# Batch 0's masks added on VectorE, batch 1's attention results on 64x64 places, and trace durations in the plan

## The chip, the cores and the metric

The kernel runs on one core of one Trainium2 chip. The core has five engines that work side by side: TensorE (matrix products), VectorE, ScalarE, GpSimd, and SyncE, whose queue issues the transfers (DMA). The metric is the time of one execution on the device in microseconds; a kernel's time is the median of its runs.

## The reference

Windowed attention over 8 batches, 8 heads, 576 tokens and a head size of 64, and then a two-layer network with a rational activation on the 4608 tokens of 512 values:

```python
scores = scale * q @ k.T                    # scale = 1/8
rel = pos[:, None] - pos[None, :]
mask_plain = (rel >= 0) & (rel < 32)        # heads 0 to 3
mask_dil = (rel >= 0) & (rel < 128) & (rel % 4 == 0)   # heads 4 to 7
attn = softmax(where(mask, scores, -1e9))
x = (attn @ v), heads side by side          # 4608 x 512
h = x @ w_in                                # 512 x 2048
P = a0 + a1*h + a2*h^2 + a3*h^3
Q = 1 + |b0|*|h| + |b1|*h^2
out = (P / (Q + 1e-6)) @ w_out              # 2048 x 512
```

q, k and v are 4-byte floats, the two weight matrices come as 8-byte floats.

## The kernel before

**Attention.** A batch is cut into six units (class `Unit`; three for the plain heads, three for the dilated ones, whose tokens are sorted by their residue so that each query sees a window of 32). A unit loads its q and k as one transfer of 448 KB (`load_qk`) and its v as one of 384 KB (`load_v`). Its scores are 24 small products for each half, 48 in all (`scores`), into columns 0 to 191 of a pair of PSUM banks: 64 rows of the array by 32 columns, moving 64 columns. The masks are a strip of 0 and -1e30 (`mask_t`, 96 KB, loaded once). For batches 0 and 1 (`on_pe`) the masks are written into the bank first, as products of an identity with the mask, and the scores are added to them; for the others VectorE adds the masks to the scores (`mask`, one or two additions a unit). Then come maximum, subtraction, exponential, sum, reciprocal (`max`, `sub`, `exp`, `sum`, `recip`) and a scaling on GpSimd (`norm`). All of batch 1's units subtract the maximum by a matmul (`KIND` 2, `sub_pe`), and one unit of batch 0 does it inside the exponential (`KIND` 1).

For batches 0 and 1 (`by_pe`) the probabilities are transposed on TensorE and copied back to SBUF (`transposes`, `place`). Later batches go through VectorE's 32x32 transposes and DRAM (`turn`, `put`, `move`).

The product with v (`av`) is again 48 matmuls, into columns 192 to 383 of a pair of banks. It has two forms. In batch 0 (`start`) v is the stationary operand: places of 64 x 64, 32 moving columns, and the result stands with the head's values on the partitions, as the network's first product needs it; `evac_hi` and `evac_lo` read it from the bank. In all other batches the probabilities are stationary: places of 64 x 32, 64 moving columns, and the result has to be turned: two 32x32 transposes on VectorE (`turn_out`), one store to DRAM (`put_out`) and four loads (`move_out`); then the evictions read the loaded tile.

An eviction splits a result into two parts, a high part `xh` (a ScalarE copy that rounds) and a low part `xl` (the difference). Both go into a batch's 512-token tiles. The last 64 tokens of a batch are left over; they go to DRAM and are worked on together as a ninth group. For batch 0's last two units (`LESS`) TensorE subtracts the high part in the bank (`less_hi`) and the low part is a copy.

Batch 0's units use three pairs of banks ("A", "B" and "att") for scores and results; the units from batch 1 on use "att" alone, for both. From batch 1 on a unit's scores are issued together with the `av` of the unit two before it, as one step of TensorE.

**Network.** 9 groups of 512 tokens by 16 slices of the inner 2048 give 144 tiles (class `Tile`). A tile has 12 matmuls of 128 x 512 for `h` (high and low parts of x and w_in), a chain of thirteen element-wise steps over ScalarE, VectorE and GpSimd (`abs` to `g_lo`), and 12 matmuls for `out`. The first eight tiles belong to batch 0, the next sixteen to batch 1, then come batch 0's other eight, and so on. Two banks hold `h`; a tile's `h` waits for the last read (`g2`) of the tile two before. Each of the 32 weight slices comes as a 512 KB transfer and is turned into a high and a low part by ScalarE, VectorE and GpSimd (`w_scale`, `w_low`, `w_join`, `w_hi`, `w_lo`).

**Order.** All steps are ops of a list scheduler (class `Plan`), which runs while the program is built. Each op has a duration for each engine that may take it, its predecessors and the buffers that it takes. At each step the plan picks, among the ops that can start within 200 ns of the earliest, the one with the lowest rank. Ranks count in tiles (`PERIOD`, 4743 ns): a network op's is its tile's number plus `LATE`, a unit's come backwards from `DUE`, a pair of numbers for each batch: the last unit's rank and the distance between units. `SLACK` moves loads and weights ahead or back. What comes out is one fixed order on each engine and on SyncE's queue; engines work in order, each instruction waiting for its predecessors by semaphores. The durations thus only decide the order.

The transfers of batch 0's units and the weights are chained in the order of their ranks. The coefficients (`lc`) and the masks (`masked`) have ranks -39.5 and -39.4 of their own.

Of the kernel before, what the change touches and what calls it, by code (L numbers as in the profile page):

```python
# [19 lines left out]
P = 128  # L20
# [18 lines left out]
DEPTH, LOADS, STAGE, AHEAD, ON_PE, BY_PE = 2, 2, 6, 6, 2, 2  # L39
# [39 lines left out]
class Plan:  # L79
# [6 lines left out]
    DMA_START, DMA_NS, DMA_RATE = 3300.0, 1750.0, 375.0  # L86
# [97 lines left out]
def tile_attention_moe(  # L184
# [72 lines left out]
    class Unit:  # L257
        def __init__(self, b, u):
            self.b, self.u, self.n = b, u, b * NU + u
            self.start, self.on_pe, self.by_pe = b == 0, b < ON_PE, b < BY_PE  # L260
            self.s_tag, self.o_tag = (START_S[u], START_O[u]) if self.start else ("att", "att")
            self.s, self.o_ps = two_banks(self.s_tag), two_banks(self.o_tag)
# [164 lines left out]
        def pieces(self):  # L427
# [14 lines left out]
            for s0, t0, step, num in segs:  # L442
# [14 lines left out]
        def src(self, cols):  # L457
            first, cnt = cols
            if not self.start:
# [4 lines left out]
        def dst(self, x, cols, d):  # L464
            return x[d].rearrange("p h (r t) -> p r h t", r=2) if self.start and cols[1] == 192 else x[d]
# [43 lines left out]
        def plan(self, by, tags):  # L509
# [10 lines left out]
            if prev:  # L520
                sc = op({"PE": 1320 + 300 * self.on_pe}, 0, lambda e: (prev.av(), self.scores()), *prev.placed, prev.lv, lq, *masks)
                clear = prev.finish(sc)
            else:
                sc = op({"PE": 1130 + 320 * self.on_pe}, 0, lambda e: self.scores(), lq, *masks)
# [5 lines left out]
            if kind == 2:  # L530
                mx = op({"DVE": 470}, 0, lambda e: self.max(True), ma)
                sb = op({"PE": 760}, 0, lambda e: self.sub_pe(), mx, identity)
                su = ex = op({"ACT": 480}, 0, lambda e: self.exp_s(), sb)
                sm = op({"DVE": 470}, 0, lambda e: self.sum(), ex)
# [3 lines left out]
            else:  # L538
                mx = op({"DVE": 470}, 0, lambda e: self.max(), ma)
                su = op({"DVE": 500}, 0, lambda e: self.sub(), mx)  # L540
                ex = op({"ACT": 425}, 0, lambda e: self.exp(), su)
                sm = op({"DVE": 470}, 0, lambda e: self.sum(), ex)
# [36 lines left out]
            if start:  # L579
                av = op({"PE": 1500}, 0, lambda e: self.av(), *self.placed, lv)  # L580
# [5 lines left out]
        def finish(self, av):  # L586
            b, start = self.b, self.start
            main, left = self.pieces()
            got = av
            if not start:  # L590
# [6 lines left out]
            low = {"DVE": sum(120 + 2 * c[1] / 0.96 for c, _ in main)}  # L597
            kl = lf = None
            if start:
                ms = eh  # L600
                if LESS[u]:
                    ms = op({"PE": sum(60 + 2 * c[1] / 1.6 for c, _ in main)}, 0, lambda e: self.less_hi(), eh, identity)
# [8 lines left out]
            else:  # L611
                low["POOL"] = sum(100 + 2 * c[1] / 0.49 for c, _ in main)
# [3 lines left out]
            if left:  # L616
                lf = op({"SP": 430 * len(left)}, self.by + 20.0, lambda e: self.put_left(), kl if start else got, dma=P * 2 * LEFT * 4 + 60000)
                left_done.append(lf)
                if start:
# [4 lines left out]
            else:  # L624
                plan.takes(got, "stage", STAGE, [x for x in (el, lf) if x])
# [8 lines left out]
            return [x for x in (el, kl) if x] if start else [to]  # L634
# [54 lines left out]
    def plan_weights(key):  # L689
# [4 lines left out]
        if wide:  # L694
            sc = op({"ACT": 600}, 0, lambda e: w_scale(key), f)
            lw = op({"ACT": 690, "POOL": 690}, 0, lambda e: w_low(key, e), f, consts)
# [350 lines left out]
```

## Time and profile before

| | |
|---|---|
| three runs | 913.51, 917.98, 916.32 us; median 916.32 |
| the profiled execution | 916.49 us, span 914.7 us |
| mean granted TensorE clock | 0.994 |
| busy share of the span | TensorE 97%, VectorE 81%, ScalarE 74%, GpSimd 51% |
| moved by DMA | 103.46 MB |

In the profile, PE is TensorE, PEld its weight loads, DVE VectorE, ACT ScalarE, POOL GpSimd, SP SyncE (SPq: its queue). L212 is the helper that issues every matmul, L209 the one for transfers, L215, L218, L221 and L224 those for activations, VectorE's and GpSimd's two-operand instructions, so the instructions are told apart by their tiles: `pair`, `pair_A` and `pair_B` are the banks of scores and results, `h` and `out` those of the network, `z` is a result that came back from DRAM, `y` a turned result on its way there, `l` the left-over columns. A row of the timeline is its start in us, its length, the engine, the instruction, its count, and in brackets the engine's idle time before it with what ended it. In grouped rows the busy us and the mean ns of one stand behind the bar.

### The profile page before, as it was taken

What the parts mean: (1) busy time and instruction counts of PE and PEld (TensorE: products, weight loads), DVE (VectorE), ACT (ScalarE), POOL (GpSimd) and SP (SyncE); (2) the same over time, 40 slices, a digit from 0 to 9 for tenths busy, and PEclk for the clock granted to TensorE, in tenths of its full rate; (3) what the DMA queues carried; (4) which work ended last, traced back from release to release, by engine and by line L of the source; (5) the groups of instructions that cost most, each with busy time, mean ns of one, the idle gap of its engine ahead of it and who ended that gap; (6) DMA issues with size and microseconds to landing.
All of it is one profiled execution on the core that took longest, in us unless ns stands there. A gap on an engine that the chain in (4) does not pass through costs nothing.

```text
span 914.7 us, 21129 instructions
## 1 busy us (share of the span) xinstructions
PE 883.2 (97%) x8153; PEld 716.1 (78%) x8153; DVE 742.3 (81%) x1312; ACT 675.4 (74%) x1092; POOL 467.7 (51%) x408
## 2 busy tenths in 40 slices
PE   5877999999999999999999999999999999999998
PEld 3755787887877878888888888888888788888876
DVE  4789999999988988788978888887779677566656
ACT  2676888877666777877787778677777688778764
POOL 2454554656635554555455555546455545444442
PEclk9989999999999999999999999999999999999999
DMA  9667460235633343334334324423333220001001
GB/s 359 240 221 249 154 234 1 99 124 190 198 99 110 110 134 118 119 111 125 115 113 127 121 83 146 129 82 85 115 95 91 61 69 1 1 1 47 0 1 47
DMA packets 85477, 103.46 MB, mean 113 GB/s; under 512 B 37376, under 2 KB 62848, under 8 KB 85376
## 3 DMA queue, kind: packets, MB, share of 16 engines
q1 hardware_dynamic: 85376, 102.11, 34.5%
q8 instruction: 64, 1.05, 0.5%
q14 instruction: 37, 0.30, 0.1%
HBM read 75.21 MB, written 26.87 MB: 112 GB/s over the span
## 4 chain that ended last, share of the span: by engine, by line
PE 75%; DVE 11%; DMA 5%; ACT 5%; issue 3%; POOL 1%; SPq 1%; DVEq 0%; POOLq 0%; ACTq 0%
PE out L212 34%; PE h L212 34%; PE pair L212 5%; DVE h L221 3%; DVE a L221 2%; DMA wi_raw<-in_w_in_dram 2%; ACT r L215 2%; DVE t L218 1%; DVE a L218 1%; DVE gl L218 1%; DMA wo_raw<-in_w_out_dram 1%; SPq L209 1%; DMA qk<-in_qk_dram 1%; ACT a L215 1%; PE pair_B L212 1%
## 5 line engine op out<-in xcount | busy, mean ns | idle before, releaser
L212 PE MATMUL h<-xh,wi 128*128 128x512 f32 x1136 | 378.1, 394 | 6.8 <-DVE a L221 6.5
L212 PE MATMUL out<-gh,wo 128*128 128x512 f32 x1136 | 353.8, 393 | 0.7 <-DVE os L218 0.7
L224 POOL TENSOR_TENSOR a<-r,a 128x512 f32<-128x512 f32 x121 | 156.6, 1294 | 241.1 <-ACT r L215 233.4
L212 PEld LDWEIGHTS h<-xh,wi 128*128 128x128 f32 x1136 | 214.5, 189 | 58.3 <-DVE a L221 12.6
L212 PEld LDWEIGHTS out<-gh,wo 128*128 128x128 f32 x1136 | 211.2, 188 | 45.9 <-DVE os L218 1.1
L212 PE MATMUL out<-gl,wo 128*128 128x512 f32 x568 | 221.8, 391 | 1.6 <-DVE gl L218 1.0
L212 PE MATMUL h<-xl,wi 128*128 128x512 f32 x568 | 222.4, 391 | 0.0
L224 POOL TENSOR_TENSOR gl<-a,gh 128x512 fp32r<-128x512 f32 x129 | 175.1, 1357 | 64.7 <-ACT gh L215 64.0
L221 DVE SCALAR_TENSOR_TENSOR h<-h,na_t,r 128x512 f32<-128x512 f32 x142 | 106.9, 753 | 111.0 <-ACT r L215 109.2
L215 ACT ACTIVATE r<-a,ln_bias 128x512 f32<-128x512 f32 x141 | 101.9, 723 | 82.8 <-POOL a L224 80.3
L215 ACT ACTIVATE r<-a,ab_t 128x512 f32<-128x512 f32 x141 | 114.7, 814 | 16.3 <-DVE a L221 14.5
L212 PEld LDWEIGHTS out<-gl,wo 128*128 128x128 f32 x568 | 106.6, 188 | 25.6 <-POOL gl L224 1.5
L212 PEld LDWEIGHTS h<-xl,wi 128*128 128x128 f32 x568 | 107.3, 189 | 21.5
L215 ACT ACTIVATE a<-h 128x512 f32<-128x512 f32 x140 | 83.5, 596 | 53.7 <-PE h L212 35.0
L215 ACT ACTIVATE t<-h,na_t 128x512 f32<-128x512 f32 x142 | 109.6, 772 | 5.0 <-PE h L212 4.6
L221 DVE SCALAR_TENSOR_TENSOR h<-t,na_t,h 128x512 f32<-128x512 f32 x142 | 107.3, 756 | 4.9
L215 ACT ACTIVATE r<-r,exp_bias 128x512 f32<-128x512 f32 x144 | 104.3, 724 | 4.7
L218 DVE TENSOR_TENSOR t<-t,h 128x512 f32<-128x512 f32 x142 | 96.6, 681 | 7.2 <-ACT t L215 7.1
L221 DVE SCALAR_TENSOR_TENSOR a<-a,r 128x512 f32<-128x512 f32 x141 | 100.2, 711 | 0.0
L221 DVE SCALAR_TENSOR_TENSOR a<-a,h 128x512 f32<-128x512 f32 x140 | 96.2, 687 | 4.8
L215 ACT ACTIVATE gh<-a 128x512 fp32r<-128x512 f32 x130 | 81.5, 627 | 23.2 <-PE out L212 14.9
L224 POOL TENSOR_TENSOR p<-p,sm 128x384 f32<-128x384 f32 x48 | 47.7, 993 | 34.3 <-DVE sm L352 28.1
(115 smaller groups left out, 712.4 us busy)
## 6 DMA issues: line engine op xcount, KB each, us to landing
qk<-in_qk_dram SPq DMA_DIRECT2D x48, 448.0 KB, 5.0
v<-in_vp_dram SPq DMA_DIRECT2D x48, 384.0 KB, 3.7
out_dram<-os SPq DMA_DIRECT2D x36, 256.0 KB, 2.3
wi_raw<-in_w_in_dram SPq DMA_DIRECT2D x16, 512.0 KB, 6.1
wo_raw<-in_w_out_dram SPq DMA_DIRECT2D x16, 512.0 KB, 6.9
results<-y SPq DMA_DIRECT2D x42, 192.0 KB, 2.4
z<-results SPq DMA_DIRECT2D x168, 48.0 KB, 2.5
turned<-u SPq DMA_DIRECT2D x36, 192.0 KB, 2.0
```

The lines of the kernel that those rows point to most:

```text
L209: pin(nc.sync.dma_start(dst, src))
L212: pin(nc.tensor.matmul(o, lhs, rhs, start=start, stop=stop, skip_group_check=free))
L215: pin(nc.scalar.activation(o, i, func, **kw))
L218: pin(nc.vector.tensor_tensor(o, x, y, op))
L221: pin(nc.vector.scalar_tensor_tensor(o, x, s, y, op0, op1))
L224: pin(nc.gpsimd.tensor_tensor(o, x, y, op))
```

## The change

- **Masks.** `on_pe` is now batch 1 alone. Batch 0's scores start without the mask products, and VectorE adds the masks to them, one or two additions a unit.
- **Batch 1's results.** A new flag `direct` (batches 0 and 1) takes the place of `start` in `av`, `pieces`, `src`, `dst` and `finish`. So batch 1's products with v use the 64x64 form, the results are split into `xh` and `xl` out of the bank, the left-over columns are copied out of it, and the transposes, the store and the loads of these six units are gone. Their low part can no longer go to GpSimd. The next scores in the pair of banks now wait for the low part and the left-over copy, where they waited for the two transposes.
- **Order of the first transfers.** The masks follow batch 0's first q and k; the coefficients, the first v and the second q and k follow the masks.
- **Plan.** Many durations are set to other values, near those of traced instructions, and the DMA model's three numbers are changed. `DUE`, `LATE` and `SLACK` have new values. `LESS` gets six zeros for batch 1.

```diff
-LESS = [0, 0, 0, 0, 1, 1]
-DUE = [(-41.16, 11.47), (-146.25, 19.43), (423.68, 72.57), (61.95, 5.87), (470.95, -17.55), (494.47, -17.25), (93.76, -24.29), (711.56, 21.96)]
-
-LATE = {"ab": -187.16, "ql": -342.11, "pl": -25.5, "qq": -118.36, "t1": -2.55, "t2": -120.77, "ln": 177.41, "ex": -496.7, "g0": -73.65, "g1": -54.63, "g2": -312.0, "gh": -189.38, "gl": 379.92, "out": 3.83}
-SLACK = {"sc": 2.49, "qk0": -51.8, "v0": -50.12, "load": 7.26, "wi": 11.43, "wo": -2.45, "w": -16.22, "gl": -5.19, "out": -6.13}
+LESS = [0, 0, 0, 0, 1, 1] + [0] * 6
+DUE = [(-96.65, 4.82), (-115.73, 29.97), (490.19, 66.11), (121.91, -6.01), (655.31, -16.58), (451.05, 0.82), (341.09, -38.16), (731.85, 36.31)]
+
+LATE = {"ab": -86.99, "ql": -477.5, "pl": 77.21, "qq": -192.99, "t1": -73.09, "t2": 3.35, "ln": 355.36, "ex": -377.4, "g0": -121.85, "g1": -6.11, "g2": -449.17, "gh": -159.19, "gl": 306.89, "out": 3.97}
+SLACK = {"sc": 2.52, "qk0": -58.23, "v0": -58.73, "load": 2.91, "wi": 1.92, "wo": -2.38, "w": -20.99, "gl": -8.34, "out": -4.45}
...
-DEPTH, LOADS, STAGE, AHEAD, ON_PE, BY_PE = 2, 2, 6, 6, 2, 2
+DEPTH, LOADS, STAGE, AHEAD, ON_PE, BY_PE, DIRECT = 2, 2, 6, 6, 2, 2, 2
...
-    DMA_START, DMA_NS, DMA_RATE = 3300.0, 1750.0, 375.0
+    DMA_START, DMA_NS, DMA_RATE = 1000.0, 1700.0, 380.0
...
-            self.start, self.on_pe, self.by_pe = b == 0, b < ON_PE, b < BY_PE
+            self.start, self.on_pe, self.by_pe, self.direct = b == 0, b == 1, b < BY_PE, b < DIRECT
...
-                        if self.start:
+                        if self.direct:
                             c0, c1 = 192 + 96 * h + 32 * i, P * i + 32 * g
                             mm(self.o_ps[64 * e : 64 * e + 64, r, c0 : c0 + 32], v_t[half, i, h, e], self.pT[half, c1 : c1 + 32], start=i == h == 0, free=True)
                         else:
...
-                    n = cnt if not self.start or cnt == 192 else min(cnt, 96 - first % 96)
+                    n = cnt if not self.direct or cnt == 192 else min(cnt, 96 - first % 96)
...
-                sc = op({"PE": 1320 + 300 * self.on_pe}, 0, lambda e: (prev.av(), self.scores()), *prev.placed, prev.lv, lq, *masks)
+                sc = op({"PE": 1320 + 700 * self.on_pe + 770 * prev.direct}, 0, lambda e: (prev.av(), self.scores()), *prev.placed, prev.lv, lq, *masks)
...
-                sb = op({"PE": 760}, 0, lambda e: self.sub_pe(), mx, identity)
+                sb = op({"PE": 950}, 0, lambda e: self.sub_pe(), mx, identity)
...
-            no = op({"POOL": 790}, 0, lambda e: self.norm(e), rc)
+            no = op({"POOL": 880}, 0, lambda e: self.norm(e), rc)
             if self.by_pe:
-                tr = op({"PE": 690}, 0, lambda e: self.transposes(), no, identity)
+                tr = op({"PE": 900 if start else 600}, 0, lambda e: self.transposes(), no, identity)
...
         def finish(self, av):
-            if not start:
+            if not direct:
                 to = op({"DVE": 590}, 0, lambda e: self.turn_out(), av)
                 po = op({"SP": 430}, 0, lambda e: self.put_out(), to, dma=P * 384 * 4)
                 got = op({"SP": 1800}, 0, lambda e: self.move_out(), po, dma=P * 384 * 4 + 160000)
...
-            if start:
+            if direct:
                 ms = eh
-                if LESS[u]:
+                if LESS[self.n]:
...
-            return [x for x in (el, kl) if x] if start else [to]
+            return [x for x in (el, kl) if x] if direct else [to]
...
-            ab = op({"ACT": 480}, k + LATE["ab"], lambda e: self.abs(), h)
+            ab = op({"ACT": 515}, k + LATE["ab"], lambda e: self.abs(), h)
...
-    lc = op({"SP": 60}, -39.5, lambda e: load(coef_t, coef), dma=3000)
-    masked.follows.append(lc)
+    lc = op({"SP": 430}, -39.3, lambda e: load(coef_t, coef), dma=3000)
...
+    masked.follows.append(first_loads[0])
+    for o in (lc, *first_loads[1:3]):
+        o.follows.append(masked)
```

More of the change, by code (lines that the diff above doesn't have):

```diff
@@ L458, in src @@
             first, cnt = cols
-            if not self.start:
+            if not self.direct:
                 return self.o[:, :384].rearrange("p (h t) -> p h t", h=2)[:, :, first : first + cnt]
@@ L464, in dst @@
         def dst(self, x, cols, d):
-            return x[d].rearrange("p h (r t) -> p r h t", r=2) if self.start and cols[1] == 192 else x[d]
+            return x[d].rearrange("p h (r t) -> p r h t", r=2) if self.direct and cols[1] == 192 else x[d]
         def evac_hi(self):
@@ L531, in plan @@
                 mx = op({"DVE": 470}, 0, lambda e: self.max(True), ma)
[L532 removed]
+                sb = op({"PE": 950}, 0, lambda e: self.sub_pe(), mx, identity)
                 su = ex = op({"ACT": 480}, 0, lambda e: self.exp_s(), sb)
[L534 removed]
+                sm = op({"DVE": 510}, 0, lambda e: self.sum(), ex)
             elif kind:
@@ L596, in finish @@
             eh = op({"ACT": sum(172 + 2 * c[1] / 1.4 * 0.75 for c, _ in main)}, 0, lambda e: self.evac_hi(), got)
-            low = {"DVE": sum(120 + 2 * c[1] / 0.96 for c, _ in main)}
+            low = {"DVE": sum(200 + 2 * c[1] / 0.9 for c, _ in main)}
             kl = lf = None
-            if start:
+            if direct:
                 ms = eh
-                if LESS[u]:
-                    ms = op({"PE": sum(60 + 2 * c[1] / 1.6 for c, _ in main)}, 0, lambda e: self.less_hi(), eh, identity)
+                if LESS[self.n]:
+                    ms = op({"PE": sum(150 + 2 * c[1] / 1.4 for c, _ in main)}, 0, lambda e: self.less_hi(), eh, identity)
                     ms.slack = 0.0
@@ L611, in finish @@
             else:
-                low["POOL"] = sum(100 + 2 * c[1] / 0.49 for c, _ in main)
+                low["POOL"] = sum(130 + 2 * c[1] / 0.45 for c, _ in main)
                 el = op(low, 0, lambda e: self.evac_lo(e), eh, lock=True)
@@ L616, in finish @@
             if left:
-                lf = op({"SP": 430 * len(left)}, self.by + 20.0, lambda e: self.put_left(), kl if start else got, dma=P * 2 * LEFT * 4 + 60000)
+                lf = op({"SP": 430 * len(left)}, self.by + 20.0, lambda e: self.put_left(), kl if direct else got, dma=P * 2 * LEFT * 4 + 60000)
                 left_done.append(lf)
-                if start:
+                if direct:
                     plan.takes(kl, "stage", STAGE, [lf])
@@ L624, in finish @@
             else:
-                plan.takes(got, "stage", STAGE, [x for x in (el, lf) if x])
+                if not direct:
+                    plan.takes(got, "stage", STAGE, [x for x in (el, lf) if x])
                 plan.takes(self.placed[0], *(("p", 2) if self.n % 2 else ("pT", 1)), [av])
@@ L695, in plan_weights @@
             sc = op({"ACT": 600}, 0, lambda e: w_scale(key), f)
-            lw = op({"ACT": 690, "POOL": 690}, 0, lambda e: w_low(key, e), f, consts)
-            jn = op({"DVE": 680}, 0, lambda e: w_join(key), sc, lw, lock=True)
+            lw = op({"ACT": 690, "POOL": 740}, 0, lambda e: w_low(key, e), f, consts)
+            jn = op({"DVE": 710}, 0, lambda e: w_join(key), sc, lw, lock=True)
             steps = [sc, lw, jn]
@@ L700, in plan_weights @@
             steps = [op({"DVE": 335}, 0, lambda e: w_copy(key), f)]
-        hi = op({"ACT": 550, "DVE": 460, "POOL": 620}, 0, lambda e: w_hi(key, e), steps[-1], lock=True)
-        lo = op({"DVE": 602, "POOL": 1280}, 0, lambda e: w_lo(key, e), hi, lock=True)
+        hi = op({"ACT": 550, "DVE": 460, "POOL": 680}, 0, lambda e: w_hi(key, e), steps[-1], lock=True)
+        lo = op({"DVE": 625, "POOL": 1350}, 0, lambda e: w_lo(key, e), hi, lock=True)
         plan.takes(steps[0], "stage", STAGE, [lo])
```

14 lines of the change are left out of this document (7 added, 7 removed).

## The prediction

> **What bounds the kernel now.** I read the busy shares first, then the engines by stretch, then the single lines of the stretches in which TensorE is not full.
>
> ```profile
> span 914.7 us, 21129 instructions
> PE 883.2 (97%) x8153; PEld 716.1 (78%) x8153; DVE 742.3 (81%) x1312; ACT 675.4 (74%) x1092; POOL 467.7 (51%) x408
> PE 75%; DVE 11%; DMA 5%; ACT 5%; issue 3%; POOL 1%; SPq 1%; DVEq 0%; POOLq 0%; ACTq 0%
> ```
>
> TensorE is busy for 883.2 of 914.7 us, and the chain of waits lies on it for 75%. So 31.5 us of TensorE's idle time are all that a better order can win, beside a faster clock and less work on TensorE. Where they lie, the engines by stretch show (length, then busy us of TensorE, its weight loads, VectorE, ScalarE, GpSimd; granted clock, DMA share):
>
> ```profile
> 0.00:40.00 40.00, 27.10 (x722) 21.71 (x722) 23.55 (x57) 17.70 (x50) 14.01 (x26) 1.00 0.78 285
> 40.00:80.00 40.00, 33.55 (x598) 26.18 (x598) 34.71 (x72) 26.07 (x46) 16.67 (x17) 0.91 0.79 274
> 80.00:120.00 40.00, 34.42 (x231) 26.78 (x230) 38.20 (x63) 34.65 (x58) 23.97 (x23) 0.96 0.45 148
> 120.00:200.00 80.00, 79.73 (x616) 63.75 (x615) 77.70 (x125) 66.09 (x106) 44.20 (x36) 1.00 0.32 112
> 300.00:400.00 100.00, 99.73 (x980) 81.25 (x979) 84.23 (x162) 75.31 (x121) 56.22 (x50) 1.00 0.40 122
> 900.00:915.00 15.00, 11.07 (x49) 8.82 (x47) 9.25 (x14) 4.68 (x7) 1.30 (x1) 1.00 0.19 72
> ```
>
> Of the idle time 24.9 us (12.9 + 6.5 + 5.6) lie before 120 us. After that TensorE is full until the last 14.7 us, where 3.6 us go to the last results. In the first 40 us no engine is full: VectorE idles 16.4 us, so the stage is set by waits. From 40 to 120 us VectorE is busy for 72.9 of 80 us (91%), and most of TensorE's stalls there end with one of its instructions:
>
> ```profile
> 48.34 0.72 PE L212 MATMUL pair<-v,pT 64*32 64x64 f32 x48 [2.46 <-ACT p L215]
> 51.69 1.65 PE L212 MATMUL pair<-mx,ident 128*128 128x192 f32 x4 [1.46 <-DVE mx L312]
> 61.08 0.92 PE L212 MATMUL pair<-mx,ident 128*128 128x192 f32 x4 [1.18 <-DVE mx L312]
> 89.19 0.50 PE L212 MATMUL h<-xh,wi 128*128 128x512 f32 x1 [3.35 <-DVE a L221]
> ```
>
> So what the change does before 120 us sets the time; whatever is saved there moves the full TensorE forward as a block. The working is made against the profiled execution, 916.49 us (span 914.7 and 1.8 us around it), which is 0.17 us above the median of 916.32.
>
> **The change, part by part. The first scores.** The queue of SyncE, its landings, and the first work that uses them:
>
> ```profile
> 0.72 0.38 SPq L209 DMA_DIRECT2D qk<-in_qk_dram  x1
> 1.16 0.42 SPq L209 DMA_DIRECT2D v<-in_vp_dram  x1
> 2.57 0.43 SPq L209 DMA_DIRECT2D mask_t<-in_mask_dram  x1
> DMA to landing us min/median/max: 3.2/6.2/10.2
> mask_t<-in_mask_dram SPq DMA_DIRECT2D x1, 96.0 KB, 4.7
> 7.31 0.48 PE L212 MATMUL pair_A<-mask_t,ident_b 128*128 128x192 bf16 x2 [7.31 <-DMA mask_t<-in_mask_dram]
> 7.72 0.97 PE L212 MATMUL pair_A<-qk 64*32 64x64 f32 x48
> 8.73 0.56 DVE L312 TENSOR_REDUCE mx<-pair_A 128x6 f32<-128x384 f32 x1 [1.43 <-PE pair_A L212]
> L218 DVE TENSOR_TENSOR pair<-pair,mask_t 128x192 f32<-128x192 f32 x36 | 13.0, 362 | 0.8
> ```
>
> The 3.2/6.2/10.2 us are the landings of batch 0's six q and k loads; the first takes 3.2 us from 0.72, so it is there at 3.9 us. TensorE waits on for the masks until 7.31, because the masks are the first matmuls of the unit. After the change the scores need q and k alone: 3.9 us, 1.0 us to the reduction's start (7.72 to 8.73), then the new mask additions (two of 0.36 us), so the first maximum starts at 5.6 instead of 8.73: 3.1 us earlier. If the masks, now issued in v's place at 1.16, take their 4.7 us again, they land at 5.9 and the maximum starts at 6.6 us: 2.1 us earlier. I take 2.6. The lower end is 0: the later units' loads arrive at the pace of the transfers (the largest landing is 10.2 us), and the head start may be lost there. The first v moves behind the masks by one issue of 0.43 us and is not used until the first unit's transposes are done, so this costs nothing.
>
> **Batch 0's masks on VectorE.** Six units issue six additions of 192 columns and three of 384 in place of twelve matmuls.
>
> ```profile
> L218 DVE TENSOR_TENSOR pair<-pair,mask_t 128x384 f32<-128x384 f32 x18 | 10.0, 556 | 0.0
> ```
>
> 6 x 0.362 + 3 x 0.556 = 3.8 us more on VectorE. TensorE loses 0.41 us for each unit (7.31 to 7.72), 2.5 us in all. In each unit's chain the one replaces the other, and VectorE's 16.4 idle us in that stage hide the sum, so I count 0; without that cover it costs 3.8.
>
> **Order of the loads.** The first units' ranks go 49 tiles forward for batch 0's last unit (its due time from -41.16 to -96.65, less 6.43 of slack), and the weights' go back by about 14 (4.77 and 9.51 of slack). Before, weights stood between them:
>
> ```profile
> 7.77 0.91 SPq L209 DMA_DIRECT2D wi_raw<-in_w_in_dram  x2
> 9.37 0.33 SPq L209 DMA_DIRECT2D qk<-in_qk_dram  x1
> 17.23 2.72 SPq L209 DMA_DIRECT2D v<-in_vp_dram  x3
> 24.29 0.97 PE L212 MATMUL pair<-qk 64*32 64x64 f32 x48
> ```
>
> Batch 0's last q and k are issued at 9.37, behind two weights, and with the longest landing of the six they are there at 19.6 us; of the three v loads from 17.23 the first is batch 0's last. Now all twelve come ahead of the first weight. The scores of that unit run only at 24.3 us (last line), since they follow the transposes of an earlier unit, so the loads alone did not hold it: what their order can win is bounded by TensorE's idle time of the first 40 us behind its first matmul, 12.9 - 7.3 = 5.6 us. What it can lose is one or two weights, 0.5 MB each at 285 GB/s (first stretch), 1.8 us each, when they are what the end of batch 0 waits for. I take 0.5 us gained, nearer to nothing, with 5.6 gained and 3.6 lost as the ends.
>
> **Batch 1 without its way through DRAM.** Away go two transposes for each unit, one store, four loads; the evictions read the bank.
>
> ```profile
> L413 DVE STREAM_TRANSPOSE y<-pair x12: 334/356/383, 42.3 to 98.0; 128x192 f32<-128x192 f32 x12
> L218 DVE TENSOR_TENSOR xl<-z,xh x7: 324/790/1370, 55.4 to 109.1; 128x256 fp32r<-128x256 f32 x3, 128x384 fp32r<-128x384 f32 x2, 128x96 fp32r<-128x96 f32 x1, 128x64 fp32r<-128x64 f32 x1
> L224 POOL TENSOR_TENSOR xl<-z,xh x2: 617/670/722, 88.9 to 89.5; 128x160 fp32r<-128x160 f32 x1, 128x192 fp32r<-128x192 f32 x1
> L218 DVE TENSOR_TENSOR xl<-pair_B,xh x4: 215/450/558, 19.0 to 27.7; 128x384 fp32r<-128x384 f32 x2, 128x192 fp32r<-128x192 f32 x1, 128x64 fp32r<-128x64 f32 x1
> L215 ACT ACTIVATE l<-pair_A x3: 198/198/238, 30.2 to 41.4; 128x32 f32<-128x32 f32 x3
> 107.77 1.91 DVE L218 TENSOR_TENSOR xl<-z,xh 128x64 fp32r<-128x64 f32 x2
> 109.58 0.68 DVE L221 SCALAR_TENSOR_TENSOR a<-a,h 128x512 f32<-128x512 f32 x1
> 110.32 0.50 PE L212 MATMUL h<-xh,wi 128*128 128x512 f32 x1 [1.21 <-DVE a L221]
> ```
>
> The transposes free 12 x 0.356 = 4.3 us of VectorE. Its subtractions were 7 x 0.79 = 5.5 us; now there are twelve pieces, all on VectorE and none on GpSimd (the pieces break at 96 columns): two at 0.55 and ten at about 0.35, some 4.6 us. That frees 0.9 more, 5.2 in all. Five copies of the left-over columns come new, 0.2 us each, on ScalarE or VectorE. VectorE is busy for 91% of this stretch and sets it, but a part of what it frees falls into its own idle time; the bounds are 0 and 5.2, and I take 0.8 of it: 4.1 us. The last lines show it: the low halves stand 1.9 us ahead of the multiplication that the next 128 x 512 matmul waits for. The latency of the way through DRAM I count at 0: batch 1's low halves end at 109.7, that multiplication at 110.3, so batch 1's readiness alone was not what TensorE waited for. Thirty issues fewer on SyncE, and 2.3 MB fewer, unblock the loads behind them; with the DMA share at 0.79 and below from 40 us on I count nothing.
>
> **Batch 1's products on 64x64 places.** One unit of each form, at the full clock, and one eviction that TensorE waits for:
>
> ```profile
> 36.45 0.90 PE L212 MATMUL pair_A<-pT,v 64*64 64x32 f32 x48
> 40.31 0.72 PE L212 MATMUL pair<-v,pT 64*32 64x64 f32 x48
> 19.58 1.50 PE L212 MATMUL pair_B<-pT,v 64*64 64x32 f32 x46 [1.22 <-DVE xl L218]
> ```
>
> 0.90 against 0.72 us, so 6 x 0.18 = 1.1 us more on TensorE; at the slow pace of the early stretch 1.50 (the third line) against 0.97 (48 matmuls of the 64x32 form at 7.72), up to 3.2. I take 1.1. The Trainium skill, TensorEngine Tiling (Array Packing), section Instruction Overhead, says that a matmul of fewer than about 60 columns costs as much as one of 60. By it, half as many places at a time and 32 columns instead of 64 would make the unit twice 0.72 us and the total 913.6 instead of 910.4 us (an estimate); the trace's 0.90 us, which is no doubling, decides.
>
> **Reordering of the rest.** The plan's durations and ranks change for all tiles. From 120 to 900 us TensorE idles for some 3.0 us (31.5 less 24.9 and 3.6; the stretch 300 to 400 above has 0.27), so there is nearly nothing to win and something to lose: bounds -2 and +5, taken as 0. The tail likewise 0.
>
> **Sum:** 916.5 - 2.6 - 0.5 - 4.1 + 1.1 = 910.4 us.
>
> **Rivals.** *The bank is held too long (slower).* Batch 1's scores and results share one pair of banks. Before, two transposes freed the results; now ScalarE's copy, VectorE's subtraction and the left-over copy must be through before TensorE may write the next scores, and TensorE is in order: all tiles' matmuls behind those scores wait too. Batch 0 shows the price once: 1.22 us until the subtraction was done. For six units that is 7.3 us, and the 1.1 us for the larger places; with the 2.6 us of the start still gained it ends at 922.3. It decides from the point where the eviction ends later than the reading of the scores that ran beside it. Against it: the units of batch 1 came some 10 us apart (transposes from 42.3 to 98.0 for six units), while a subtraction takes 0.56 us at most (558 ns above). Chance 0.16.
>
> *VectorE's sum binds (no change).* If VectorE is the bound from the first scores on, its new 3.8 us count and its 5.2 us are nearly given back: 1.4 us gained, less 1.1 on TensorE: 916.2; with half of the start's 2.6 us kept 914.9. For it speaks the 91%; against it 16.4 idle us before 40. The change not doing what it says belongs here: were the second q and k load what batch 0 waits for, the masks' place would be worth nothing. Chance 0.18.
>
> *The first stage closes up (faster still).* All of batch 0's data are there early, and the first stage's idle time shrinks by half of the 5.6 us, 2.8, VectorE's full 5.2 us count, and the gap of 3.35 us ahead of 89.19 goes with the slow clock after it. The first three give 916.5 - 3.1 - 2.8 - 5.2 + 1.1 = 906.5; with half of the 3.35 us gap beyond VectorE's share 904.8. Chance 0.16.
>
> **How the numbers follow.** My forecast has 0.50. A measurement of this kernel can tell about 0.5% from no change, so faster ends at 911.7 and slower begins at 920.9. The forecast's own range is 906 to 915, and about seven tenths of its chance lie below 911.7. Faster: 0.36 and the last rival's 0.16, together 0.52. Same: the rest of the forecast, 0.14, and nearly all of the 0.18: 0.31. Slower: the bank's 0.16, and 0.01 for a reordering that costs its 5 us on top of a bound VectorE: 0.17. The range for 8 in 10 goes from 902 (the last rival with its 2 us from the later reordering) to 921, which leaves out most of the slower case.
>
> **What would show it.** Right: the first scores near 4 us and the first maximum near 6; batch 0's six q and k loads all ahead of the first weight; VectorE's share from 40 to 120 us below 91% or the same work ending some 5 us sooner; the stalls at 61 and 89 us shorter. Wrong: TensorE idle ahead of batch 1's scores with the subtraction or the left-over copy as the releaser; TensorE idle for more than 3 us between 120 and 900; the first 128 x 512 matmul not before 41.9 us, where it begins now.
>
> ```profile
> 41.89 0.50 PE L212 MATMUL h<-xh,wi 128*128 128x512 f32 x1
> ```

## The result, and the profile after

The kernel after takes 924.99 us (median of eight runs, 920.88 to 929.41) against 915.94 for the kernel before (eight runs beside it, 913.51 to 918.58): ratio 1.0101, 95% interval 1.0084 to 1.0119. It is slower, by 9.3 us (0.0101 of 916), where 910.4 was forecast; differences below that rest on a ratio are worked out like this one. The profiled execution took 925.27 us. Its page and the engines by stretch (length, then busy us of TensorE, its weight loads, VectorE, ScalarE, GpSimd; granted clock, DMA share, GB/s):

```profile
span 923.5 us, 21101 instructions
PE 889.1 (96%) x8141; PEld 721.6 (78%) x8141; DVE 726.1 (79%) x1296; ACT 675.4 (73%) x1097; POOL 481.4 (52%) x427
PE 75%; DVE 6%; ACT 4%; DMA 3%; POOL 1%; issue 1%; SPq 1%; ACTq 0%; POOLq 0%; DVEq 0%
```

```profile
0.00:40.00 40.00, 26.06 (x705) 20.92 (x706) 25.56 (x64) 20.03 (x51) 14.11 (x26) 1.00 0.89 324
40.00:80.00 40.00, 33.03 (x569) 25.65 (x568) 29.26 (x60) 27.05 (x59) 20.16 (x21) 0.92 0.71 232
80.00:120.00 40.00, 38.32 (x255) 30.89 (x254) 36.69 (x61) 35.09 (x61) 25.25 (x23) 0.99 0.37 134
120.00:200.00 80.00, 79.30 (x617) 63.81 (x616) 74.89 (x122) 64.92 (x103) 51.54 (x43) 1.00 0.31 104
200.00:300.00 100.00, 96.90 (x960) 78.45 (x959) 86.67 (x163) 66.96 (x108) 48.42 (x48) 0.98 0.44 137
300.00:400.00 100.00, 98.43 (x1062) 79.40 (x1061) 82.20 (x158) 73.62 (x119) 54.73 (x48) 1.00 0.40 124
400.00:500.00 100.00, 98.85 (x976) 80.32 (x976) 81.42 (x154) 74.32 (x118) 53.72 (x47) 1.00 0.37 115
```

Three things are to be seen. VectorE did get lighter, 742.3 to 726.1 us, and from 40 to 120 us its share fell from 91% to 82% (29.26 + 36.69 of 80). That did not put TensorE ahead: by 120 us it has done the attention of the same units in both kernels, but only 201 recorded 128x512 matmuls where it had done 211; at one in 0.23 us that is 2.3 us behind. And behind 120 us holes have come: 0.7, 3.1, 1.6 and 1.2 us in the last four rows, with a lower clock in one of them. The kernel before has 0.3, 1.8, 0.3 and 0.0 us there; of its four rows these two have not been shown yet:

```profile
200.00:300.00 100.00, 98.16 (x1060) 78.55 (x1059) 90.16 (x169) 71.64 (x116) 51.34 (x49) 1.00 0.49 155
400.00:500.00 100.00, 100.00 (x983) 81.80 (x982) 85.20 (x158) 75.43 (x121) 54.22 (x44) 1.00 0.38 116
```

So of the 8.8 us by which the span grew (914.7 to 923.5) some 6.5 lie behind 120 us, where none of the moved work is left. At 250 us both kernels have done 729 of these matmuls (the kernel after one unit's scores fewer); at 400 us it is 1298 against 1325, which is 6.2 us. Most of the loss falls between these two points.

TensorE's timeline of the early part (start, us, matmuls; in brackets the idle time ahead and what ended it):

```profile
3.91 0.97 PE L212 MATMUL pair_A<-qk 64*32 64x64 f32 x48 [3.91 <-DMA qk<-in_qk_dram]
...
7.88 0.97 PE L212 MATMUL pair<-qk 64*32 64x64 f32 x48 [3.00 <-DMA qk<-in_qk_dram]
...
16.18 0.86 PE L212 MATMUL pair_B<-pT,v 64*64 64x32 f32 x21 [2.40 <-issue]
...
47.12 1.65 PE L212 MATMUL pair<-mx,ident 128*128 128x192 f32 x4 [1.12 <-ACT xh L215]
...
48.32 0.88 PE L212 MATMUL h<-xh,wi 128*128 128x512 f32 x1
...
53.52 0.90 PE L212 MATMUL pair<-pT,v 64*64 64x32 f32 x48
...
57.75 0.92 PE L212 MATMUL pair<-mx,ident 128*128 128x192 f32 x4 [1.91 <-DVE xl L218]
```

VectorE's and SyncE's timelines:

```profile
5.72 0.56 DVE L312 TENSOR_REDUCE mx<-pair_A 128x6 f32<-128x384 f32 x1
```

```profile
16.21 0.33 SPq L209 DMA_DIRECT2D wo_raw<-in_w_out_dram  x1
```

The first scores start at 3.91 us and the first maximum at 5.72, as forecast, but the second unit's wait 3.00 us for their q and k, and the first 128x512 matmul comes at 48.32 instead of 41.89 us. In batch 1 the softmax now waits for evictions out of the same pair of banks (47.12 and 57.75).

The largest hole behind 120 us, on TensorE, in the chain of waits and in SyncE's queue:

```profile
256.74 0.94 PE L212 MATMUL pair<-v,pT 64*32 64x64 f32 x44 [3.08 <-DMA pT<-turned]
```

```profile
251.65 5.04 DMA pT<-turned
...
256.74 1.58 PE pair L212 x74
258.32 4.38 PE h L212 x12
...
266.55 2.95 PE h L212 x12
```

```profile
248.19 0.38 SPq L209 DMA_DIRECT2D turned<-u  x1
248.61 1.44 SPq L209 DMA_DIRECT2D os<-part  x3
250.21 0.88 SPq L209 DMA_DIRECT2D left<-z  x2
251.14 0.47 SPq L209 DMA_DIRECT2D turned<-u  x1
251.65 1.25 SPq L209 DMA_DIRECT2D pT<-turned  x2
```

Three fetches of partial sums (256 KB each) are issued between a unit's store of transposed probabilities and the load that brings them back; that load takes 5.04 us, and the twelve matmuls behind the hole take 4.38 us instead of 2.95.

### The profile page after: what moved, and what is told of

Same layout as the page of the kernel before. It is cut to its first block, busy times and chain, and to the rows that moved or that the text cites. A ratio compares the mean times of both kernels' runs of the same rounds, so it can differ in the third digit from the quotient of the medians.

```text
span 923.5 us, 21101 instructions
## 1 busy us (share of the span) xinstructions
PE 889.1 (96%) x8141; PEld 721.6 (78%) x8141; DVE 726.1 (79%) x1296; ACT 675.4 (73%) x1097; POOL 481.4 (52%) x427
## 4 chain that ended last, share of the span: by engine, by line
PE 75%; DVE 6%; ACT 4%; DMA 3%; POOL 1%; issue 1%; SPq 1%; ACTq 0%; POOLq 0%; DVEq 0%
PE h L212 36%; PE out L212 35%; PE pair L212 4%; ACT r L215 2%; DVE a L221 2%; DVE h L221 2%; DMA z<-results 1%; SPq L209 1%; DMA results<-y 1%; POOL a L224 1%; DVE t L218 1%; DMA pT<-turned 1%; ACT t L215 1%; ACT a L215 0%; ACT xh L215 0%
## 5 line engine op out<-in xcount | busy, mean ns | idle before, releaser
L224 POOL TENSOR_TENSOR gl<-a,gh 128x512 fp32r<-128x512 f32 x133 | 179.2, 1347 | 44.6 <-ACT gh L215 41.9
L215 ACT ACTIVATE gh<-a 128x512 fp32r<-128x512 f32 x126 | 79.1, 628 | 27.5 <-PE out L212 20.5
L224 POOL TENSOR_TENSOR p<-p,sm 128x384 f32<-128x384 f32 x48 | 44.6, 930 | 34.0 <-DVE sm L352 31.3
```

Source lines behind the costliest of these rows:

```text
L215: pin(nc.scalar.activation(o, i, func, **kw))
L224: pin(nc.gpsimd.tensor_tensor(o, x, y, op))
```

## The experiments

Two theories stood against each other: that the loss lies in the **parts** of the change (F in the expectations), or in the new **written-out order** of all tiles (E). All ratios are to runs of the kernel before on the same chip; 0.001 is 0.92 us.

**x1: one spot of the order.** Three of the four fetches of partial sums go behind the next load of transposed probabilities; nothing else moves.

```diff
+        first = named["part"][:3]
+        at = self.order.index(first[-1])
+        behind = next(o for o in self.order[at:] if getattr(o, "name", None) == "move")
+        for o in first:
+            self.order.remove(o)
+        at = self.order.index(behind) + 1
+        self.order[at:at] = first
```

> The changed kernel with one thing moved: three of the four loads that fetch batch 0's partial sums back (256 KB each) are issued behind the loads of the next unit's transposed probabilities instead of ahead of them; every other engine keeps its order. Theory A (the order that the new ranks gave costs the time behind 120 us): the stall of 3.08 us at 256.7 us, and the slow clock behind it (12 matmuls of h in 4.38 instead of 2.95 us), go: 3 to 5 us faster than the changed kernel, 920 to 922 us. Rival B (the time is lost in the first stage, and later stalls only take up slack that another wait would take): within 1.5 us of the changed kernel's 925.

920.09 us, 1.0052 [1.0034, 1.0071]: 4.5 us of the 9.3 are gone with three transfers. TensorE's timeline at the place:

```profile
254.53 0.65 PE L227 MATMUL pair<-v,pT 64*32 64x64 f32 x42 [0.33 <-DMA pT<-turned]
```

**x2 and z4: the evictions out of the shared banks.** Batch 1's evictions go behind the exponential of the unit that shares the banks. In x2 this also moved the last two units' evictions behind the first network matmuls that read them: that version reads those parts of x before they are written. z4 moves batch 1's own units alone (the condition `b == 1`).

```diff
+        for ex, evict in self.pairs:
+            at = self.order.index(ex)
+            early = [o for o in evict if self.order.index(o) < at]
+            for o in early:
+                self.order.remove(o)
+            at = self.order.index(ex) + 1
+            self.order[at:at] = early
...
+            if prev and prev.direct and b == 1:
+                plan.pairs.append((ex, prev.evictions))
```

> The changed kernel with batch 1's evictions (high part, low part, left-over copy) moved behind the exponential of the unit whose scores share the pair of banks; TensorE's order is unchanged. Theory C (in the changed kernel the eviction and the softmax of that pair of banks wait for each other in turn: high part after the maximum, subtraction after the high part, low part after the subtraction, exponential after the low part): TensorE's waits of 1.12 us at 47.1 and 1.91 us at 57.8 go, the exponentials start about 1.5 us earlier each, 2 to 4 us faster, 921 to 923 us. Rival D (the next scores then wait for the eviction instead): the waits reappear ahead of the next scores, 925 or more.

> The kernel after with the evictions of batch 1's own units alone moved behind the exponential of the unit that shares the banks; the order on TensorE and GpSimd is the same. Theory C (the wait of the exponential for the low part is what costs before 120 us): 921 to 923 us against 925, with TensorE's stalls of 1.1 and 1.9 us at 47 and 58 gone. Rival D (the bank is then held longer, and the next scores wait instead): 925 us or more, with new stalls ahead of batch 1's results or scores that end with the subtraction.

x2: 926.56 us, 1.0105 [1.0057, 1.0153]; z4: 923.60 us, 1.0090 [1.0060, 1.0120], neither apart from the kernel after, and z4 lies between what its two theories gave. The waits did not go, they moved ahead of the next results. TensorE in x2:

```profile
55.72 0.90 PE L224 MATMUL pair<-pT,v 64*64 64x32 f32 x48 [1.55 <-DVE xl L230]
...
73.04 0.90 PE L224 MATMUL pair<-pT,v 64*64 64x32 f32 x48 [1.77 <-ACT l L227]
```

**v3: x1 and z4 together.**

```diff
+        first = named["part"][:3]
...
+        for ex, evict in self.pairs:
...
```

> The kernel after with the edits of x1 (three part-sum fetches behind the next pT loads) and z4 (batch 1's evictions behind the exponential) together. If the two costs are separate: 925.0 - 4.9 - 1.4 = 918.7 us. If the waits only give way to the next in line: 920 us, as x1 alone. Not below before in either case, if batch 1's part costs 2 to 3 us by itself as w2 has it.

922.17 us, 1.0051 [1.0035, 1.0067], as x1 alone (1.0052): the second edit gave nothing more.

**x3: the order alone.** The kernel before, its due times nudged at random by about 0.3 of a tile; the same work.

```diff
-DUE = [(-41.16, 11.47), (-146.25, 19.43), ...]
+DUE = [(-41.38, 11.54), (-146.53, 19.47), ...]
-LATE = {"ab": -187.16, "ql": -342.11, ...}
+LATE = {"ab": -187.17, "ql": -341.48, ...}
```

> The kernel before, with every rank moved by some 0.3 of a tile at random (DUE and LATE) and nothing else changed; the plan's own end goes from 907.3 to 918.9 us. Theory E (the times of both kernels are set by how well the ranks were fitted to their plan, and any other fit costs several us): 922 to 930 us, stalls of TensorE behind 120 us or a longer first stage. Rival F (the order matters little, the parts of the change matter): 914 to 918 us.

924.80 us, 1.0108 [1.0084, 1.0133]. Another order of the same work is worth the whole result.

**x4: the kernel after with the ranks of the kernel before** (DUE, LATE and SLACK).

```diff
-DUE = [(-96.65, 4.82), (-115.73, 29.97), ...]
+DUE = [(-41.16, 11.47), (-146.25, 19.43), ...]
...
```

> The changed kernel, its new durations kept, with the ranks (DUE, LATE, SLACK) of the kernel before; the plan's own end goes from 911.5 to 922.2 us. Theory E (fit of the ranks): 930 to 938 us, more than either kernel. Rival F (the parts of the change cost the time, the ranks little): 922 to 928 us. If the new ranks are the bad part: 912 to 918 us.

931.88 us, 1.0189 [1.0149, 1.0229]. The ranks fit one set of durations; with the new durations the old ranks are worse still.

**y0 to y3: every version with ranks searched anew.** The durations of the kernel after in all four, and ranks from equally long searches; without the parts, with the masks alone, with batch 1's results alone, with both. The ranks shown are y0's; each has its own.

```diff
-    DMA_START, DMA_NS, DMA_RATE = 3300.0, 1750.0, 375.0
+    DMA_START, DMA_NS, DMA_RATE = 1000.0, 1700.0, 380.0
...
-DUE = [(-41.16, 11.47), (-146.25, 19.43), ...]
+DUE = [(-43.35, 5.23), (-116.64, 77.9), ...]
```

> None of the change's parts but its durations: the program's steps are those of the kernel before, the plan has the new durations, and DUE, LATE and SLACK were searched anew from the ranks of the kernel before for the plan's own end (912.8 us by it). One of four kernels with the same search and the same starting ranks. Theory E (the fit of the order sets the time; the parts are worth 2 us or less each): all four within some 5 us of each other, and the plan's own ends (912.8, 916.3, 912.3, 913.7) don't foretell which is first; this one 918 to 926. Rival F (the parts themselves cost the 9 us): this one 913 to 917.

> Batch 0's masks on VectorE and the new order of the first loads alone, batch 1's results as before; the same durations and the same search (plan's own end 916.3). Theory E: within 5 us of the one without the parts, 920 to 928. Rival F, if the masks are the costly part: 5 to 9 us above the one without.

> Batch 1's results on 64x64 places and out of the bank alone, masks and first loads as before; the same durations and search (plan's own end 912.3). Theory E with the chain in the bank pair (which the plan does not know): 1 to 4 us above the one without, 919 to 929. Rival F, if this is the costly part: 5 to 9 us above. If the DRAM way's removal is worth my predicted 4 us: 3 to 4 us below it.

> All parts of the change, the same durations and search (plan's own end 913.7), another fit than the changed kernel's. Theory E: 918 to 930, several us from the changed kernel's 925 either way although nothing but ranks differs. Rival F: 923 to 927.

922.54 (1.0060 [1.0044, 1.0076]), 924.12 (1.0079), 923.89 (1.0068) and 925.81 us (1.0093 [1.0073, 1.0113]). With an order found in the same way, both parts together cost 3.3 us (925.81 - 922.54), and the order of y0 by itself, without any part, costs 5.5 us. How much of the 3.3 us is the luck of four searches no run tells: the nudge of x3 alone moved the time by 9.9 us.

**z1 and w1: the masks in the old order.** The kernel before with its ranks and durations; each addition goes right ahead of its unit's maximum, the mask matmuls are dropped, the load is second. w1 also moves the scaling of the coefficients, which in z1 stood first on VectorE, behind the first subtraction (the last pair of lines).

```diff
-            on_pe = self.on_pe
+            on_pe = self.on_pe and not self.start
...
-    mx = op({"DVE": 470}, 0, lambda e: self.max(), ma)
+    mx = op({"DVE": 470}, 0, lambda e: (self.start and self.mask(), self.max()), ma)
...
             load(t, qk[self.n])
+            if self.n == 0:
+                load(mask_t, mask)
...
-    su = op({"DVE": 500}, 0, lambda e: self.sub(), mx)
+    su = op({"DVE": 500}, 0, lambda e: (self.sub(), self.n or make_na()), mx)
```

> The kernel before with its plan's numbers and so its written-out order untouched; only batch 0's masks move to VectorE in place (each addition right ahead of the maximum of its unit, the twelve mask matmuls dropped) and the masks' load goes from the fifth to the second transfer. Theory 1 (the forecast's term of the first scores holds when nothing else is reordered): 2.6 us less than before, 913.3 against 915.9, with the first scores at 4 us. Theory 2 (the head start is lost before 120 us whatever the order, as in the kernel after): within 1.5 us of before, with TensorE's idle time before 120 us again at 22 us or more.

> As the run z1 (the kernel before in its own order, batch 0's masks on VectorE, their load second), and the scaling of the coefficients, which stood first on VectorE and held its first mask addition until the coefficients landed at 8.4 us, moved behind the first unit's subtraction. Theory 1 (in z1 only that instruction hid the head start): the first maximum near 6 us and the end 2.1 to 2.6 us below before, 914.0 to 914.5 against 916.6. Theory 2 (the second unit's q and k land at 8.2 us and take the head start anyway): the first maximum near 6 us, but the second unit's scores at 8.2 us as in z1, and the end within 1.5 us of before.

z1: 916.68 us, 0.9995 [0.9981, 1.0010]; w1: 916.72 us, 1.0009 [0.9994, 1.0025]: nothing, with the first scores more than 3 us earlier. The page of w1 and its TensorE:

```profile
PE 880.4 (96%) x8141; PEld 714.9 (78%) x8141; DVE 745.7 (82%) x1321; ACT 675.0 (74%) x1092; POOL 466.0 (51%) x408
```

```profile
3.73 0.97 PE L212 MATMUL pair_A<-qk 64*32 64x64 f32 x48 [3.73 <-DMA qk<-in_qk_dram]
...
8.41 0.97 PE L212 MATMUL pair<-qk 64*32 64x64 f32 x48 [3.71 <-DMA qk<-in_qk_dram]
...
12.74 0.96 PE L212 MATMUL pair<-qk 64*32 64x64 f32 x48 [1.15 <-DMA qk<-in_qk_dram]
...
28.91 0.65 PE L212 MATMUL pair_A<-pT,v 64*64 64x32 f32 x16 [2.77 <-issue]
...
41.68 0.50 PE L212 MATMUL h<-xh,wi 128*128 128x512 f32 x1
```

The head start is handed back at the second and the fourth unit's loads and in a stop of 2.77 us without a releaser; the first 128x512 matmul comes 0.2 us earlier than before.

**z2 and z3: batch 1's results in the old order, as it was meant.** The evictions stand where the transposes stood.

```diff
-    to = op({"DVE": 590}, 0, lambda e: self.turn_out(), av)
+    to = op({"DVE": 590}, 0, lambda e: self.evict() if self.direct else self.turn_out(), av)
...
-    po = op({"SP": 430}, 0, lambda e: self.put_out(), ...)
+    po = op({"SP": 430}, 0, lambda e: self.direct or self.put_out(), ...)
```

> The kernel before with its plan's numbers and order untouched; only batch 1's results run on 64x64 places and are evicted out of the bank, high part, low part and left-over columns together at the place where the transposes stood. Theory 1 (the forecast's two terms, -4.1 and +1.1): 913 us. Theory 2 (the bank held by the chain of maximum, high part, subtraction, low part, exponential costs some 1.2 us a unit and the larger places 1.1 us): 916 to 922 us, with TensorE's stalls before batch 1's work ending with the copy or the subtraction of the pair of banks.

> Both parts in the kernel before with its plan's numbers and order untouched. Theory 1 (the forecast's terms add: -2.6, -4.1, +1.1): 910.3 us, which would put the whole loss on the new plan. Theory 2 (the parts themselves cost, or gain nothing): 915 to 922 us. In the refitted plans the two parts came to +3.3 us together.

927.19 us, 1.0116 [1.0101, 1.0132], and 929.41 us, 1.0141 [1.0125, 1.0156]. The numbers look like Theory 2, but the stalls don't lie in batch 1. TensorE in z2:

```profile
200.76 0.50 PE L212 MATMUL h<-xh,wi 128*128 128x512 f32 x1 [2.17 <-DVE a L221]
...
252.12 0.87 PE L212 MATMUL pair<-v,pT 64*32 64x64 f32 x42 [2.10 <-DVE sm L349]
```

The condition of both expectations was not met: the pieces of 96 columns changed the durations of batch 1's evictions in the plan, and with them the order of some 400 lines of VectorE's 1219. By 120 us TensorE is even ahead in z2, 221 of the 128x512 matmuls against 211 in the kernel before, with the attention of the same units done; then 15.5 us of idle time follow, where the kernel before has 6.6.

**w2 and w3: the same in the true old order.** The plan costs the evictions as before, so only batch 1's own instructions differ (with `plan` set, `pieces` gives the old pieces for batch 1); w3 has w1's edits as well.

```diff
-        def pieces(self):
+        def pieces(self, plan=False):
+            direct = self.direct and not (plan and self.b)
...
-            main, left = self.pieces()
+            main, left = self.pieces(True)
```

> As the run z2, but with the plan's durations of batch 1's evictions held at their old values too: the pieces of 96 columns had changed them in z2, and the plan had laid out some 400 of VectorE's 1219 lines otherwise, so z2 had not kept the order as its expectation said. Here only batch 1's own instructions differ. Theory 1 (the forecast's -4.1 and +1.1): 913.6 us against 916.6. Theory 2 (the bank pair's chain costs by itself): 918 to 924 us. Theory E (z2's 10.6 us were its new order): well below z2's 927.2, within 3 us of before.

> w1 and w2 together: every part of the change in the order of the kernel before. Theory 1 (all of the forecast's terms): 910.9 us against 916.6. Theory E with Theory 2 of w1: within 3 us of before. Theory 2 of w2: 918 us or more.

w2: 919.02 us, 1.0029 [1.0014, 1.0043]; w3: 919.89 us, 1.0039 [1.0024, 1.0054]. The same work as z2 and z3, 8.0 and 9.3 us faster by its order. The time of w2 fits its Theory 2 and its Theory E alike. The parts cost 3.6 us in the old order, and their interval lies clear of the 1.0084 where that of the kernel after begins: of the 9.3 us, 5.7 are left for the new order, if the two add. What w2's 2.7 us are, the engines in the stretch of 42 to 92 us show, first of the kernel before, then of w2, and w2's page and TensorE's timeline:

```profile
42.00:92.00 50.00, 39.27 (x526) 30.37 (x527) 44.74 (x84) 35.66 (x63) 22.30 (x24) 0.91 0.72 245
```

```profile
42.00:92.00 50.00, 39.16 (x530) 30.30 (x517) 38.69 (x73) 33.34 (x63) 19.73 (x20) 0.88 0.60 207
```

```profile
PE 885.5 (97%) x8153; PEld 718.8 (78%) x8153; DVE 736.6 (80%) x1305; ACT 675.0 (74%) x1100; POOL 465.9 (51%) x406
```

```profile
49.31 1.44 PE L212 MATMUL pair<-pT,v 64*64 64x32 f32 x48 [2.75 <-ACT p L215]
...
53.73 1.65 PE L212 MATMUL pair<-mx,ident 128*128 128x192 f32 x4 [1.64 <-DVE mx L313]
...
64.55 0.92 PE L212 MATMUL pair<-mx,ident 128*128 128x192 f32 x4 [1.75 <-DVE mx L313]
...
66.31 0.90 PE L212 MATMUL pair<-pT,v 64*64 64x32 f32 x48
...
92.40 0.79 PE L212 MATMUL h<-xh,wi 128*128 128x512 f32 x1 [4.09 <-DVE a L221]
```

VectorE works 6.1 us less there, and TensorE idles as long as before (10.8 against 10.7 us). Four waits at the same places are longer, 2.75, 1.64, 1.75 and 4.09 us where they were 2.46, 1.46, 1.18 and 3.35; three others that ended with VectorE are shorter or gone, 0.68 us for 1.11 near 80 us and none for 1.00 at 83.24 and 1.21 at 110.32. Over the whole span 2.3 of the 2.7 us are TensorE's busy time (885.5 against 883.2) and 0.4 us its idle time; the granted clock in this stretch was 0.88 against 0.91.

Where VectorE's freed time went, its waits from 42 to 112 us show (us in total, times, longest), first of the kernel before, then of w2:

```profile
DVE xl L218 <- ACT xh L215: 0.6, 2, 0.5
```

```profile
DVE xl L218 <- ACT xh L215: 8.3, 5, 2.4
```

The low parts now stand in VectorE's line where the transposes stood. The transposes needed TensorE's results alone; the low parts need ScalarE's high parts too, and VectorE waits 8.3 us for them, more than it was freed of.

**v1 and v2: the loads' pace.** w1 and w3, with each of the first three v loads behind the q and k of the second unit after it.

```diff
             load(t, qk[self.n])
+            if self.n - 2 in later:
+                load(*later.pop(self.n - 2))
...
-            load(self.v, vp[self.n])
+            if self.n < 3:
+                later[self.n] = self.v, vp[self.n]
+            else:
+                load(self.v, vp[self.n])
```

> As the run w1, and the first three v loads each moved behind the q and k of the second unit after it, so that q and k of the first four units are issued among the first seven transfers. Theory L (the pace of the loads takes the head start in w1: the second unit's scores wait 3.71 us for q and k, the fourth's 1.15): second scores near 6 us, fourth near 11, the first 128x512 matmul 1 to 2 us before 41.7, the end 914.5 to 915.5 us against 916.2. Rival (what sets the first stage from some 15 us on is the order of VectorE's instructions and the weights' loads): earlier scores, the first 128x512 matmul within 0.7 us of 41.7, the end within 0.8 us of before.

> As the run w3 (every part in the order of the kernel before) with the loads of v1. Theory L: 1 to 2 us below w3's 919.9. Rival: the same as w3 within 0.8 us. In both cases batch 1's part still costs its 2 to 3 us, so that it stays above before.

v1: 913.83 us, 0.9970 [0.9958, 0.9981]; v2: 917.70 us, 1.0011 [0.9998, 1.0024]: 0.0039 and 0.0028 below w1 and w3, so 3.6 and 2.6 us. TensorE in v1:

```profile
4.02 0.97 PE L212 MATMUL pair_A<-qk 64*32 64x64 f32 x48 [4.02 <-DMA qk<-in_qk_dram]
...
6.56 0.97 PE L212 MATMUL pair<-qk 64*32 64x64 f32 x48 [1.57 <-DMA qk<-in_qk_dram]
...
25.98 0.65 PE L212 MATMUL pair_A<-pT,v 64*64 64x32 f32 x16 [0.83 <-issue]
...
38.77 0.50 PE L212 MATMUL h<-xh,wi 128*128 128x512 f32 x1
```

The second scores come 1.9 us earlier than in w1, the first 128x512 matmul 2.9 us. v1 is faster than both kernels, by 0.3% of the one before: a part of the change, the masks, in the old order with the loads set to it. No run has these loads without the masks on VectorE, so the two are not told apart.

## Why the prediction was wrong, step by step

**What bounds the kernel.** That the idle time to be won lies before 120 us was right: v1 wins there. That VectorE sets that stretch, so that four fifths of what it is freed of are won, was read from its 91%, and the share does not show it. w2 takes 5.7 us off VectorE (742.3 to 736.6), and TensorE's idle time stays: VectorE waits for ScalarE instead. The runs do not refute it either, since TensorE does get ahead in z2.

**First scores, -2.6.** The times were right (3.91 us, first maximum at 5.72 us for 3.9 and 5.6 forecast) and the gain came to nothing, the lower bound, for the reason named there: as long as the first v goes ahead of them, the second unit's q and k hold its scores until 7.9 to 8.4 us. So taking 2.6 failed. In v1, with those loads earlier, the masks and the loads together are worth 2.7 us.

**Masks on VectorE, 0.** Nothing speaks against it, though w1 measures it together with the first scores: in w1 TensorE works 2.8 us less (880.4), VectorE 3.4 us more (745.7), and the time is that of before.

**Order of the loads, -0.5.** All twelve loads did come ahead of the first weight, and that weight is issued at 16.21 instead of 7.77 us. The first 128x512 matmul stands 6.4 us later in the kernel after, and 2.3 us of that are left at 120 us. It is mostly the order and not the parts: with the parts in the old order that matmul starts at 40.49 us (w3), with the new durations and no part at 45.92 us (y0). How much is the weights and how much the other order of the tiles no run tells apart.

**Batch 1, -4.1.** This step failed in the old order. The 5.2 us freed were well counted (5.7); of the two bounds, 0 and 5.2, w2 gives 0. What the step left out is the wait for ScalarE's high part that the new evictions bring into VectorE's line, 8.3 us in w2; that this wait is what took the gain is read from the trace, no run removes it. In z2, with nearly the same wait (7.2 us) but another order, TensorE is ten 128x512 matmuls ahead of the kernel before at 120 us (w2 is sixteen behind, 195 against 211). That is 2.3 us, near the 3.0 us that this term and the next forecast together, and it is lost again behind 120 us.

**64x64 places, +1.1.** The price is right (0.90 us, at 53.52 in the kernel after and 66.31 in w2). In w2 five units took 0.90 and one, at the slow pace behind a wait of 2.75 us, 1.44: 1.6 us more than six times 0.72. TensorE's whole work grew by 2.3. The Trainium skill's rule (TensorEngine Tiling (Array Packing), section Instruction Overhead) would have made it twice 0.72; no unit at the full clock took that.

**Reordering of the rest, 0.** This is the step that failed most: some 6.5 us behind 120 us by the two profiles, 5.7 us as the remainder beside w3, past its bound of +5. The 3 us of idle time from 120 to 900 us were read as "nearly nothing to win", which was right; in the kernel after they are 7.8 us. The loss was taken as 0, though nothing in the working held it there. x3 shows that a nudge of the ranks costs 9.9 us, x1 that three misplaced transfers cost 4.5.

In the forecast's own terms the runs put 3.6 us on the parts in the old order and leave 5.7 us for the new one. That these make 9.3 us proves nothing, since the second is the remainder. In the kernel after itself, level in 128x512 matmuls with the one before at 250 us, what the parts cost is not shown.

**The rivals.** "The bank is held too long" had the sign, at 922.3 us, but its mechanism is far smaller than its price: in w2 the waits at the shared banks come to 6.1 us (2.75 + 1.64 + 1.75) against 5.1 before (2.46 + 1.46 + 1.18), 1.0 us and not 7.3. In the kernel after two waits that end with an eviction come to 3.0 us (1.12 + 1.91), and moving the evictions moves the waits without a gain clear of noise (x2, z4, v3). "VectorE's sum binds" gave about no change, against 9.3 us measured; whether VectorE binds in that stretch stays open. "The first stage closes up" needs the loads' order of v1, which the change does not have.

**The signs named ahead.** All of those for "wrong" came: TensorE idle with the subtraction as the releaser (1.91 us at 57.75, ahead of the maximum's matmul and not of the scores), 7.8 us idle from 120 to 900 us, the first 128x512 matmul after 41.9 us. But those for "right" came for the most part too: the first scores at 3.91 and the first maximum at 5.72 us, all six q and k ahead of the first weight, VectorE's share at 82%. They tested whether the parts did what they should, not whether the order behind them held.

## What to carry to other kernels

A head start at the first instruction is worth what the second unit's data allow, so follow the next two or three loads before counting it. A busy share of 91% doesn't show that an engine is the bound; ask which waits would end earlier if it were lighter, and what its new instructions will wait for in its line. Where the order of a program comes out of a search, a change of its durations is a change of every place in it: price that with a version in the old order and a nudged one before the parts are judged.

## What was not expected of the hardware

**TensorE stops at fixed counts of instructions.** The long stops whose releaser is "issue" fall on fixed counts. Ahead of the matmul behind such a stop the trace has 222 matmuls in the kernel after (2.40 us), 350 and 477 in the kernel before (1.18 and 1.17 us), 476 in w1 (2.77 us) and in v1 (0.83 us): some 127 matmuls apart, 254 with their weight loads. All such stops of over 1 us in the traces of this case stand at these counts. The page of the kernel after has a queue for instructions:

```profile
q8 instruction: 64, 1.05, 0.5%
```

64 packets of 16 KB fit the 16,282 matmuls and weight loads, 254 to a packet. In w1 the DMA queues of the microsecond from 26 us show one of them, in the stop that lasts from 26.14 to 28.91 us:

```profile
q8 instruction: 1, 0.02, 6.4%
```

So the likely cause is a block of instructions that comes late behind the data; no run here tried it. The Trainium skill (Runtime: NRT & Kernel Launch, section Instruction fetch mechanics) describes such blocks of 256 instructions and calls their cost mostly hidden; if they are the cause, in this stage it is not.

**A hole costs more than its length.** Behind the hole of 3.08 us at 256.74 the next twelve matmuls took 4.38 us instead of 2.95, 1.4 us more, with a granted clock of 0.67 from 258 to 263 us and 1.00 from 266 to 270 us.
